# First half of the rows of w1 and w2 by ordinary products; weight sums on VectorE; pairs of rows in turns

## The chip, the core and the metric

One core of a Trainium2 chip. The metric is device microseconds of one execution, the median of three timed runs. PE is TensorE's matmul, PEld its weight load, DVE VectorE, ACT ScalarE, POOL GpSimd, SP the engine that issues the DMAs.

## What is computed

Causal attention (2 batches, 12 heads, 448 tokens, head size 64), then two feed-forward blocks without a nonlinearity in the first and with a squared ReLU in the second:

```python
attn = softmax(mask(q @ k.T / sqrt(64))) @ v      # (2, 12, 448, 64)
x = attn.transpose(0, 2, 1, 3).reshape(896, 768)
a = x @ w1                                        # (896, 1024)
b = x @ w2                                        # (896, 1024)
x = (a * b) @ w3 @ w_out                          # (896, 768)
h = x @ w_in2                                     # (896, 2048)
out = maximum(h, 0) ** 2 @ w_out2                 # (896, 768)
```

All weights arrive as 64-bit floats (two 32-bit words each).

## The kernel before

**Number format.** Each fp32 operand is kept as two tiles, a high part (ACT casts it to fp32r) and a low part (DVE or POOL subtracts the high part from the value). A product of 128 contraction rows is three matmuls (high·high, high·low, low·high). A raw 64-bit weight becomes fp32 by one ACT and two DVE instructions (`convert`, L92, L93, L98; in the changed kernel L93, L94, L99) into one of six slots of `xs`; a *unit* (half a row block, 128x384) is then split into one of eight slots of `ring` by an ACT cast (L87) and a DVE subtraction (L96). In the changed kernel these are L88 and L97.

**Stages, in PE's order.** (1) Attention for 12 pairs of heads; in its gaps PE forms w3 @ w_out (`w_half`), collected in `wraw` and written to DRAM. (2) a and b, from `w1` and `w2`: eight row blocks ("rows", 128 outputs each) of either matrix. (3) `h`: (a*b) times the product of stage 1. (4) Four groups, each of four rows of w_in2 (tiles `win_*`, then `gT`) and of 168 matmuls `o` with w_out2. 

**Stage 2 and the first part of 4 use Strassen's scheme (the form with seven products)** on a pair of rows: contraction halves, and token halves (the two batches) give a 2x2 block problem. A product is nine matmuls of 448 columns (three contraction blocks, three parts). Chains: products 1 and 2 add up in bank a, 6, 7 and 4 in bank b, 5 and 3 in bank c; between two products of one chain DVE reads the bank (L696, L699, L701, L704, L709), so the next product of the chain waits for that read. The weight operands are A11, A12, A22 (units of the rows) and S1 to S4 (sums of halves of rows); the x operands are the blocks B11, B21, B22 and T1 to T4 (sums of B blocks). Before, POOL makes S1 to S4 of a pair with four instructions (`sums`, L240, L241, L243, L244) into two further slots of `xs`, so that a pair takes four of the six slots.

**Order.** PE follows `plan`, in which `TWO` gives the order of the 14 products of two pairs (P of w1, Q of w2; or two pairs of w_in2). `pump` fills the queues of the other engines by a count of what is free: a unit is made as soon as the ring slot of the eighth unit before it has been read for the last time. In stages 2 to 4 a scheduler orders ACT, DVE and POOL; each of them then works strictly in that order. Raw weights come through two buffers (`raw`), so a load starts when the raw tile two before it has been turned into fp32.

Of the kernel before, what the change touches and what calls it, by code (L numbers as in the profile page):

```python
# [8 lines left out]
F32 = mybir.dt.float32  # L9
# [8 lines left out]
def attention_moe_moe2(ctx: ExitStack, tc: tile.TileContext, qk, v, w1, w2, w3, w_out, w_in2, w_out2, out):  # L18
# [25 lines left out]
    LEAD = 5  # L44
    TAIL = 1
    LENT = (("wout", 2), ("wout", 3))
    PAUSE = 64
# [36 lines left out]
    def convert(a=None, y=None, b=None, t=None, x=None):  # L84
# [12 lines left out]
        if a:  # L97
            nc.vector.scalar_tensor_tensor(  # L98
                y.bitcast(U32), y.bitcast(U32), 3, low, op0=ALU.logical_shift_left, op1=ALU.bitwise_or)  # L99

    def halves(x):
# [18 lines left out]
    plan = []  # L120
# [5 lines left out]

    for d in range(KF // 2):
        two_pairs([("w1", 2 * d), ("w2", 2 * d)])
# [21 lines left out]
    def wide(u):  # L150
        return u[0] in ("W", "wout2")
# [14 lines left out]
    def needs(u):  # L166

        if wide(u):
            return u, slice(0, DM)
        name, (nm, m) = u  # L170
        lo, hi = slice(0, HN), slice(HN, DM)
        return {
            "A11": ((nm, m), lo), "A12": ((nm, m), hi), "A22": ((nm, m + 1), hi),
            "S2": (("S12", nm, m), lo), "S1": (("S12", nm, m), hi),
            "S3": (("S34", nm, m), lo), "S4": (("S34", nm, m), hi),
        }[name]

    items, readers = [], {}
    for u in units:
        key = u if wide(u) else u[1]  # L180
        if wide(u):
            group = [u]
        else:
            nm, m = key
            group = [(nm, m), (nm, m + 1), ("S12", nm, m), ("S34", nm, m)]
# [5 lines left out]
        if not wide(u):  # L191
            for it in group[:2]:
                for s in group[2:]:
                    if s not in readers[it]:
                        readers[it].append(s)

    n_unit = {u: i for i, u in enumerate(units)}

    def done_with(it):

        return max(n_unit[r] if r in n_unit else done_with(r) for r in readers[it])

# [31 lines left out]
    def sums(it):  # L234
        which, nm, m = it
        p, q = in_slot((nm, m)), in_slot((nm, m + 1))
        t = in_slot(it)
        a, b = t[:, :HN], t[:, HN:]
        if which == "S12":
            nc.gpsimd.tensor_tensor(b, q[:, :HN], q[:, HN:], op=ALU.add)  # L240
            nc.gpsimd.tensor_tensor(a, b, p[:, :HN], op=ALU.subtract)  # L241
        else:
            nc.gpsimd.tensor_tensor(a, p[:, :HN], q[:, :HN], op=ALU.subtract)  # L243
            nc.gpsimd.tensor_tensor(b, p[:, HN:], in_slot(("S12", nm, m))[:, :HN], op=ALU.subtract)  # L244

    def simple_items():

        while (it := next_item()) and it[0] not in source:
# [7 lines left out]
            items_made.add(it)  # L256
            made["item"] += 1

    def item_of():
# [5 lines left out]
        items_made.add(it)  # L265
        return {"a": it, "y": in_slot(it)}

    def unit_of(at):
# [4 lines left out]
        it, cols = needs(u)  # L273
        if it not in items_made:
            return {}
# [34 lines left out]
    with (  # L310
# [7 lines left out]
    ):  # L318
        wraw = attw.tile([P, KF, DM], F32, tag="W", name="wraw")
        ident = attc.tile([P, P], F32, tag="ident", name="ident")  # L320
# [106 lines left out]
        def x_parts(p):  # L427
# [11 lines left out]
            elif (b, h) == (1, 0):  # L439
                two_parts(xB["B11"][:, 0, k], xB["B11"][:, 1, k], x)  # L440
                xf["T2", k] = f_tile(f"xT2_{k}")
                nc.vector.tensor_tensor(xf["T2", k], x, xf["T3", k], op=ALU.add)
                t1 = xf["T1", k] = xf.pop(("B12", k))
                nc.vector.tensor_tensor(t1, t1, x, op=ALU.subtract)
            else:
# [10 lines left out]
        def w_half(g, i, n):  # L456
# [3 lines left out]
            for f in range(NB):  # L460
# [8 lines left out]
            dst = wraw[:, i, cols]  # L469
            if g > 0:  # L470
                nc.vector.tensor_tensor(dst, acc, dst, op=ALU.add)
                if n == 1:
                    nc.sync.dma_start(out=w_dram[i], in_=wraw[:, i])
            else:
# [242 lines left out]
    more_blocks("x", xB)  # L717
    for n in ("T2", "T1", "T3"):
        for k in range(KH):
            x = xf[n, k] if n == "T2" else xf.pop((n, k))  # L720
            block_parts(xB, n, k, x, nc.gpsimd if n == "T3" else None)
    for k in range(KH):
        x = xf.pop(("B21", k))
        block_parts(xB, "B21", k, x)
        t2 = xf.pop(("T2", k))
        nc.vector.tensor_tensor(t2, x, t2, op=ALU.subtract)
        block_parts(xB, "T4", k, t2)

# [44 lines left out]
    def g_out(nm, m, b, x, in_psum):  # L773
# [49 lines left out]
    w12 = Pairs(xB, ab_out)  # L823
    gs = None
    with tc.manual_schedule(engines={ET.PE}):
        pump(-1)
        for at, (kind, what, which, used) in enumerate(plan):
            if kind == "product":
                nm, m = which
# [74 lines left out]
```

## Time and profile before

| | |
|---|---|
| median of three timed runs | 587.75 us (583.67 to 588.22) |
| profiled execution | 585.41 us, of which 583.6 us from the first to the last instruction |
| PE busy | 546.6 us (94%) |
| DVE, ACT, POOL busy | 406.8, 312.4, 282.0 us (70%, 54%, 48%) |
| mean granted TensorE clock | 0.982 of 2.4 GHz |
| stage 1, attention with w3 @ w_out | 0 to 166.90 us |
| stage 2, products of w1 and w2 | 166.90 to 292.34 us |
| stage 3, h | 292.34 to 350.70 us |
| stage 4, four groups of win and o | 350.70 to 580.3 us |

A stage begins at PE's first matmul of it. PE being busy 94% of the span is an average: stage 3 has no gap at all, stage 2 has its gaps at the seams and between products of one chain. Which gaps these are, and what ended them, stands in the timeline of PE.

### The profile page before, as it was taken

Reading aid. Unit: us, or ns where it says so; the run is one execution under the profiler, and the core shown is the slowest. Engines: PE = TensorE matmul, PEld = TensorE weight load, DVE = VectorE, ACT = ScalarE, POOL = GpSimd, SP = SyncE. Lnnn points to the kernel's source line nnn. Section 1 sums busy time; section 2 is a strip of 40 time slices with the busy share of each in tenths; the row PEclk is TensorE's granted clock in tenths of the full one; section 3 lists DMA queues with packets and bytes.
Section 4 is the critical chain, followed back from the end, with each engine's and each line's share of the span. In section 5 each row is a group of like instructions: output and inputs, shape, how many; then the busy total and the mean of one; then the engine's idle time right before and its main releaser. Section 6 shows DMA issues by size and latency. Waiting matters only on the chain.

```text
span 583.6 us, 8340 instructions
## 1 busy us (share of the span) xinstructions
PE 546.6 (94%) x3004; PEld 485.7 (83%) x3004; DVE 406.8 (70%) x770; ACT 312.4 (54%) x685; POOL 282.0 (48%) x231
## 2 busy tenths in 40 slices
PE   7899989999948988989999999989989998999997
PEld 5668768778837977888999999889989997999997
DVE  5987887878559998787533658863896489538622
ACT  6788777667566453534322546942683258315900
POOL 3378667766535583847253462651164206511510
PEclk9999999999987999898999999999999998999999
DMA  8854554544343333242430304630443045303022
GB/s 298 299 192 137 175 157 156 141 168 125 142 135 107 111 108 109 77 140 83 135 109 0 109 0 116 210 108 1 151 173 108 1 157 169 109 0 109 1 81 110
DMA packets 18153, 70.27 MB, mean 120 GB/s; under 512 B 1920, under 2 KB 4224, under 8 KB 18112
## 3 DMA queue, kind: packets, MB, share of 16 engines
q1 hardware_dynamic: 18112, 69.74, 36.3%
q8 instruction: 24, 0.39, 0.3%
q14 instruction: 17, 0.14, 0.1%
HBM read 63.83 MB, written 5.90 MB: 119 GB/s over the span
## 4 chain that ended last, share of the span: by engine, by line
PE 59%; DVE 15%; ACT 10%; DMA 6%; POOL 5%; issue 4%; DVEq 0%; ACTq 0%; POOLq 0%
PE o L65 18%; PE h L65 10%; PE w L65 8%; DVE ring L96 4%; DVE xs L98 3%; PE s L65 3%; DMA raw_wout<-in_w_out 3%; ACT xs L92 3%; PE x L65 2%; PE pp L408 2%; ACT p L380 2%; ACT pt L412 2%; PE w_6b L65 2%; PE w_4b L65 2%; DMA raw_w<-in_w 2%
## 5 line engine op out<-in xcount | busy, mean ns | idle before, releaser
L96 DVE TENSOR_TENSOR ring<-xs,ring 128x384 fp32r<-128x384 f32 (+1 forms) x140 | 118.4, 858 | 34.4 <-ACT ring L87 34.2
L87 ACT CAST ring<-xs 128x384 fp32r<-128x384 f32 (+1 forms) x140 | 78.4, 577 | 96.9 <-PE o L65 44.9
L390 POOL TENSOR_SCALAR p<-p,st 112x448 f32<-112x448 f32 (+1 forms) x84 | 95.7, 1156 | 53.8 <-ACT pt L412 20.6
L65 PE MATMUL o<-ring,gT 128*128 128x384 f32 x672 | 117.9, 335 | 2.6 <-POOL gT L69 2.6
L65 PEld LDWEIGHTS o<-ring,gT 128*128 128x128 f32 x672 | 116.5, 188 | 3.6 <-POOL gT L69 3.3
L240 POOL TENSOR_TENSOR xs<-xs 128x384 f32<-128x384 f32 x16 | 18.9, 1181 | 98.7 <-DVE ring L96 80.8
L380 ACT ACTIVATE p<-p,st 112x448 f32<-112x448 f32 (+1 forms) x96 | 49.7, 530 | 27.8 <-DVE st L373 27.6
L65 PE MATMUL h<-abT,ring 128*128 128x448 f32 x288 | 58.5, 365 | 0.0
L65 PEld LDWEIGHTS h<-abT,ring 128*128 128x128 f32 x288 | 54.1, 188 | 4.3
L811 DVE TENSOR_TENSOR acc<-o,acc 128x384 f32<-128x384 f32 x42 | 21.4, 550 | 35.1 <-PE o L65 35.0
L373 DVE CUSTOM_DVE_ANT_0 p<-s,mask 112x448 f32<-112x448 f32 (+1 forms) x96 | 36.5, 443 | 6.9 <-PE s L65 6.9
L65 PE MATMUL w<-hl_wout,w 128*128 128x384 f32 x192 | 36.2, 340 | 0.9 <-ACT xB L447 0.9
L92 ACT ACTIVATE xs<-raw_w 128x768 f32<-128x768 f32 (+1 forms) x30 | 24.6, 819 | 20.5 <-DVE ring L96 13.3
L65 PEld LDWEIGHTS w<-hl_wout,w 128*128 128x128 f32 x192 | 32.9, 188 | 2.4 <-ACT xB L447 1.1
L65 PE MATMUL s<-qk 64*112 64x112 f32 (+3 forms) x192 | 28.5, 432 | 4.5 <-DMA qk<-in_qk 4.4
L98 DVE SCALAR_TENSOR_TENSOR xs<-xs,raw_w 128x768 uint32<-128x768 uint32 (+1 forms) x30 | 27.1, 904 | 5.8 <-ACT xs L92 5.7
L408 PE MATMUL pp<-ident,p 112*112 112x112 f32 x240 | 27.4, 262 | 3.7 <-DVE st L373 2.9
L408 PEld LDWEIGHTS pp<-ident,p 112*112 112x112 f32 x240 | 23.6, 134 | 7.9 <-POOL p L390 2.8
L92 ACT ACTIVATE xs<-raw_wout 128x768 f32<-128x768 f32 x24 | 22.0, 925 | 13.7 <-DMA raw_wout<-in_w_out 11.6
L412 ACT COPY pt<-pp 112x336 f32<-112x336 f32 (+1 forms) x72 | 27.7, 477 | 1.8 <-PE pp L408 1.8
L65 PEld LDWEIGHTS s<-qk 64*112 64x112 f32 x192 | 15.9, 185 | 15.1 <-issue 6.0
L65 PE MATMUL w<-ring,w 128*128 128x384 f32 x144 | 27.9, 343 | 0.3 <-DVE w L96 0.3
(307 smaller groups left out, 1078.8 us busy)
## 6 DMA issues: line engine op xcount, KB each, us to landing
raw_wout<-in_w_out SPq DMA_DIRECT2D x24, 768.0 KB, 4.4
raw_w<-in_w SPq DMA_DIRECT2D x16, 768.0 KB, 4.4
raw_win<-in_w_in SPq DMA_DIRECT2D x16, 768.0 KB, 4.3
raw_w<-in_w SPq DMA_DIRECT2D x16, 512.0 KB, 4.2
qk<-in_qk SPq DMA_DIRECT2D x12, 448.0 KB, 5.1
w_dram<-wraw SPq DMA_DIRECT2D x8, 384.0 KB, 3.3
xs<-w_dram SPq DMA_DIRECT2D x8, 384.0 KB, 3.4
v<-in_v SPq DMA_DIRECT2D x12, 224.0 KB, 3.3
```

The costliest lines, as they stand in the source:

```text
L65: return nc.tensor.matmul(o, l, r, start=start, stop=stop, **more)
L87: nc.scalar.copy(t[0], x)
L92: nc.scalar.activation(y, high.bitcast(F32), AF.Prelu, scale=2.0 ** -112, alpha=-2.0 ** 32)
L96: nc.vector.tensor_tensor(t[1], x, t[0].bitcast(F32), op=ALU.subtract)
L98: nc.vector.scalar_tensor_tensor(y.bitcast(U32), y.bitcast(U32), 3, low, op0=ALU.logical_shift_left, op1=ALU.bitwise_or)
L240: nc.gpsimd.tensor_tensor(b, q[:, :HN], q[:, HN:], op=ALU.add)
L373: nc.vector.tensor_tensor_reduce(e, ps[j, i], mask[:, S - (i + 1) * CP:], QS, 3.0e38, ALU.add, ALU.min, st_t[p][:, 0, j, i:i + 1],)
L380: nc.scalar.activation(e, e, AF.Exp, bias=st_t[p][:, 0, j, i:i + 1], scale=-1.0, accum_out=st_t[p][:, 1, j, i:i + 1])
L390: engine.tensor_scalar(e, e, st[:, 3, i:i + 1], None, ALU.mult)
L408: nc.tensor.transpose(x[:CP, o:o + CP], pt[:, off[i] + c * CP:off[i] + (c + 1) * CP], ident[:CP, :CP],)
L412: nc.scalar.copy(t[:, coff[g[0]]:coff[g[0]] + o], x[:CP, :o])
L811: nc.vector.tensor_tensor(a, o, a, op=ALU.add)
```

## The change

**Rows.** The first four rows of w1 and of w2 (`ORDINARY = 4`) no longer go through Strassen's scheme: each is multiplied with the four blocks B11, B12, B21, B22 of x, four products of nine matmuls. For the first four rows (w1_0, w2_0, w1_1, w2_1) the products with B11 and B22 come first, for all of them, and those with B12 and B21 after. B12 takes the tile that T4 had; T4 (`xlast`) is made at the last row, in another tile. Rows 4 to 7 stay in pairs.

**Order of products.** `TWO` is now 1P 1Q 6P 6Q 5P 5Q 7P 7Q 3P 3Q 2P 2Q 4P 4Q, for w1/w2 and for w_in2.

**Sums.** DVE makes the four sums of a pair; S3 and S4 overwrite halves of the rows themselves, so a pair takes three slots of `xs`. S4 is made once A11 is in the ring. POOL makes none.

**Smaller edits.** `wraw` is eight tiles. The T blocks of x are made in another order, T1 from the parts of B11 after the attention, and DVE makes the low parts that POOL made for T3. Of the low parts of `gT` DVE makes two of eight in a group, POOL the rest.

```diff
+    ORDINARY = 4
...
-    TWO = ("P1", "P6", "P5", "Q1", "P7", "P3", "Q6", "Q5", "P2", "P4", "Q7", "Q3", "Q2", "Q4")
+    TWO = [x + n for n in "1657324" for x in "PQ"]
...
-    for d in range(KF // 2):
+    rows = [(nm, i) for i in range(ORDINARY) for nm in ("w1", "w2")]
+    for row in rows[:4]:
+        for u, n in zip(row_units(row), ("B11", "B22")):
+            plan.append(("row", n, row, [u]))
+    for i, row in enumerate(rows):
+        u, u2 = row_units(row)
+        if i >= 4:
+            plan += [("row", "B11", row, [u]), ("row", "B12", row, [u])]
+            plan += [("row", "B21", row, [u2]), ("row", "B22", row, [u2])]
+        else:
+            plan += [("row", "B12", row, [u]), ("row", "B21", row, [u2])]
+    for d in range(ORDINARY // 2, KF // 2):
         two_pairs([("w1", 2 * d), ("w2", 2 * d)])
...
-            nc.gpsimd.tensor_tensor(b, q[:, :HN], q[:, HN:], op=ALU.add)
-            nc.gpsimd.tensor_tensor(a, b, p[:, :HN], op=ALU.subtract)
...
-            nc.gpsimd.tensor_tensor(a, p[:, :HN], q[:, :HN], op=ALU.subtract)
-            nc.gpsimd.tensor_tensor(b, p[:, HN:], in_slot(("S12", nm, m))[:, :HN], op=ALU.subtract)
...
+        tt = nc.vector.tensor_tensor
+        tt(t[:, HN:], q[:, :HN], q[:, HN:], op=ALU.add)
+        tt(t[:, :HN], t[:, HN:], p[:, :HN], op=ALU.subtract)
+        tt(q[:, :HN], p[:, :HN], q[:, :HN], op=ALU.subtract)
...
+            if (nm, m) not in s4_made and ("A11", (nm, m)) in hls:
+                p = in_slot((nm, m))
+                nc.vector.tensor_tensor(p[:, :HN], p[:, HN:], in_slot(it)[:, :HN], op=ALU.subtract)
...
-        wraw = attw.tile([P, KF, DM], F32, tag="W", name="wraw")
+        wraw = [attw.tile([P, DM], F32, tag=f"W{i}", name=f"wraw{i}") for i in range(KF)]
...
-        two_parts(*(g_t[m % 4][:, s, b * S:(b + 1) * S] for s in range(2)), r, nc.gpsimd)
+        two_parts(*(g_t[m % 4][:, s, b * S:(b + 1) * S] for s in range(2)), r,
+                  nc.gpsimd if m % 4 < 2 or b == 0 else nc.vector)
...
+                for k in range(KH):
+                    for s, r in ((0, 0), (0, 1), (1, 0)):
+                        mm(o, t[s][:, k * P:(k + 1) * P], xB[what][:, r, k],
+                           not stop and k == 0 and (s, r) == (0, 0), stop and k == KH - 1 and (s, r) == (1, 0))
+                if stop:
+                    ab_out(nm, m, int(b), row_banks.pop((nm, m, b)), True)
```

ACT's queue at the end of the attention, before (x_1833 is the attention output of the last pair but one, the `xs` casts are units of w1 and w2, the pt copies serve the last pair):

```order
L87 CAST ring<-xs 128x384
L92 ACTIVATE xs<-raw_w_1_1632 128x768 [waits DMAHW4_49,DVE_49]
L87 CAST ring<-xs 128x384 [waits Pool_49]
L447 COPY xB_1_1842<-x_1833 128x448 [waits PE_49]
L87 CAST ring<-xs 128x384
L92 ACTIVATE xs<-raw_w_0_1679 128x768 [waits DMAHW7_49]
L87 CAST ring<-xs 128x384 [waits DVE_49]
L412 COPY pt_1867<-pp_0_1868 112x448 [waits PE_49]
```

The same place in the changed kernel:

```order
L88 CAST ring<-xs 128x384
L93 ACTIVATE xs<-raw_w_0_1636 128x768 [waits DMAHW4_49,DVE_49]
L88 CAST ring<-xs 128x384
L467 COPY xB_1_1842<-x_1833 128x448 [waits PE_49]
L88 CAST ring<-xs 128x384 [waits DVE_49]
L93 ACTIVATE xs<-raw_w_1_1683 128x768 [waits DMAHW7_49]
L88 CAST ring<-xs 128x384
L434 COPY pt_1867<-pp_0_1868 112x448 [waits PE_49]
```

The cast ahead of the copy of x no longer waits for POOL; the cast behind the copy now waits for DVE.

PE's first products of stage 2, before (`w1_0a` is bank a of the pair w1 rows 0 and 1; the second name is the block of x):

```order
L65 MATMUL w1_0a_2017<-xB11_72,ring_70 128x448 x9
L65 MATMUL w1_0b_2037<-xT2_1965,ring_70 128x448 x9
L65 MATMUL w1_0c_2053<-xT1_1964,ring_70 128x448 x9
L65 MATMUL w2_0a_2067<-xB11_72,ring_70 128x448 x9
L65 MATMUL w1_0b_2037<-xT3_1966,ring_70 128x448 x9
```

And in the changed kernel (`w1_0_True` and `w1_0_False` are the two banks of row 0 of w1; xT4 is here B12):

```order
L66 MATMUL w1_0_True_2044<-xB11_72,ring_70 128x448 x9
L66 MATMUL w1_0_False_2055<-xB22_73,ring_70 128x448 x9
L66 MATMUL w2_0_True_2065<-xB11_72,ring_70 128x448 x9
L66 MATMUL w2_0_False_2075<-xB22_73,ring_70 128x448 x9
L66 MATMUL w1_1_True_2085<-xB11_72,ring_70 128x448 x9
L66 MATMUL w1_1_False_2095<-xB22_73,ring_70 128x448 x9
L66 MATMUL w2_1_True_2105<-xB11_72,ring_70 128x448 x9
L66 MATMUL w2_1_False_2115<-xB22_73,ring_70 128x448 x9
L66 MATMUL w1_0_False_2055<-xT4_1968,ring_70 128x448 x9
```

Before, the second product needed T2; now the first eight need only B11 and B22.

POOL's queue between the products of the first group of stage 4 and its `o` matmuls, before (`gT0_3` is the last tile that `o` asks for):

```order
L69 TENSOR_TENSOR gT0_0_3292<-r0_1_3446,gT0_0_3292 128x448 [waits Activation_49]
L240 TENSOR_TENSOR xs_71<-xs_71 128x384 [waits DVE_49]
L243 TENSOR_TENSOR xs_71<-xs_71 128x384 [waits DVE_49]
L241 TENSOR_TENSOR xs_71<-xs_71 128x384 [waits Pool_49]
L69 TENSOR_TENSOR gT0_1_3293<-win2_0s1_3306,gT0_1_3293 128x448 [waits Activation_49]
L244 TENSOR_TENSOR xs_71<-xs_71 128x384 [waits Pool_49]
L69 TENSOR_TENSOR gT0_3_3295<-win2_2s3_3431,gT0_3_3295 128x448 [waits PE_49,Activation_49]
L69 TENSOR_TENSOR gT0_2_3294<-win2_2s2_3419,gT0_2_3294 128x448 [waits Activation_49]
```

In the changed kernel:

```order
L70 TENSOR_TENSOR gT0_1_3291<-win2_0s3_3370,gT0_1_3291 128x448 [waits PE_49,Activation_49]
L70 TENSOR_TENSOR gT0_3_3293<-win2_2s3_3389,gT0_3_3293 128x448 [waits PE_49,Activation_49]
L70 TENSOR_TENSOR gT0_0_3290<-win2_0s2_3332,gT0_0_3290 128x448 [waits Activation_49]
L70 TENSOR_TENSOR gT0_2_3292<-win2_2s2_3351,gT0_2_3292 128x448 [waits Activation_49]
L70 TENSOR_TENSOR gT0_0_3290<-r0_1_3475,gT0_0_3290 128x448 [waits Activation_49]
```

The four sums are gone from this queue, and `gT0_3` stands second in it.

## Rows read from the trace of the kernel before

**Rows 1.** The page, part 1: busy us (share of the span) xinstructions

```profile
PE 546.6 (94%) x3004; PEld 485.7 (83%) x3004; DVE 406.8 (70%) x770; ACT 312.4 (54%) x685; POOL 282.0 (48%) x231
```

**Rows 2.** Timeline, PE, stage 2: start us, us, engine, operation, count, idle before

```profile
159.74 2.35 PE L65 MATMUL w<-hl_wout,w 128*128 128x384 f32 x12 [0.90 <-ACT xB L447]
163.71 2.54 PE L65 MATMUL x<-pt,v 112*64 112x448 f32 x16 [1.62 <-ACT pt L412]
166.90 0.43 PE L65 MATMUL w_0a<-ring 128*128 128x64 f32 x2 [0.65 <-ACT xB L447]
...
174.78 0.74 PE L65 MATMUL w_0b<-xT,ring 128*128 128x448 f32 x1 [5.57 <-ACT xT L68]
...
290.51 1.99 PE L65 MATMUL w_6b<-xT,ring 128*128 128x448 f32 x9
292.34 7.86 PE L65 MATMUL h<-abT,ring 128*128 128x448 f32 x38
```

**Rows 3.** Waits of PE: who waited for whom, us in total, times, longest

```profile
PE o L65 <- POOL gT L69: 2.6, 2, 2.3
PE win_10b L65 <- DVE win_10s L701: 2.6, 1, 2.6
PE w_2b L65 <- DVE w_2s L696: 2.4, 1, 2.4
PE w_4b L65 <- DVE w_4s L701: 2.2, 1, 2.2
PE w_2b L65 <- DVE w_2s L701: 2.0, 1, 2.0
```

**Rows 4.** Timeline, PE, stage 4

```profile
350.70 1.99 PE L65 MATMUL win_0a<-hB,ring 128*128 128x448 f32 x9
...
496.09 29.28 PE L65 MATMUL o<-ring,gT 128*128 128x384 f32 x168
525.21 0.33 PE L65 MATMUL win_12a<-ring 128*128 128x64 f32 x2
...
550.98 29.29 PE L65 MATMUL o<-ring,gT 128*128 128x384 f32 x168
```

**Rows 5.** Timeline, all engines, end of the attention

```profile
153.81 0.55 DVE L93 TENSOR_SCALAR raw_w<-raw_w 128x768 uint32<-128x768 uint32 x1
154.28 0.55 DVE L96 TENSOR_TENSOR ring<-xs,ring 128x384 fp32r<-128x384 f32 x1
154.75 0.95 DVE L98 SCALAR_TENSOR_TENSOR xs<-xs,raw_w 128x768 uint32<-128x768 uint32 x1
...
158.74 0.51 ACT L87 CAST ring<-xs 128x384 fp32r<-128x384 f32 x1 [5.75 <-POOL xs L241]
159.16 0.53 ACT L447 COPY xB<-x 128x448 f32<-128x448 f32 x1
```

**Rows 6.** Timeline, all engines, ahead of the wait of w_2b

```profile
207.23 1.34 POOL L244 TENSOR_TENSOR xs<-xs 128x384 f32<-128x384 f32 x1
...
207.74 1.99 PE L65 MATMUL w_2c<-xT,ring 128*128 128x448 f32 x9
...
209.06 0.91 ACT L92 ACTIVATE xs<-raw_w 128x768 f32<-128x768 f32 x1 [1.26 <-POOL xs L244]
...
210.00 1.93 DVE L98 SCALAR_TENSOR_TENSOR xs<-xs,raw_w 128x768 uint32<-128x768 uint32 x1 [1.02 <-ACT xs L92]
...
213.25 0.61 DVE L696 TENSOR_TENSOR w_2s<-w_2b,w_2s 128x448 f32<-128x448 f32 x1
```

**Rows 7.** Lines by form, stage 2: count | busy us, mean ns | idle before

```profile
L96 DVE TENSOR_TENSOR ring<-xs,ring 128x384 fp32r<-128x384 f32 x51 | 42.8, 847 | 5.8 <-ACT ring L87 5.8
...
L69 POOL TENSOR_TENSOR abT<-w_0s,abT 128x448 fp32r<-128x448 f32 x3 | 4.4, 1470 | 1.9 <-ACT abT L68 1.9
...
L69 DVE TENSOR_TENSOR xB<-xB,xB 128x448 fp32r<-128x448 f32 x3 | 4.0, 1396 | 0.0
...
L69 DVE TENSOR_TENSOR xT<-xT,xT 128x448 fp32r<-128x448 f32 x6 | 3.5, 614 | 0.0
```

More of the change, by code (lines that the diff above doesn't have):

```diff
@@ L184, in attention_moe_moe2 @@
             nm, m = key
[L185 removed]
+            group = [(nm, m)] if u[0] in "LH" else [(nm, m), (nm, m + 1), ("S", nm, m)]
         for it in group:
@@ L190, in attention_moe_moe2 @@
         readers[needs(u)[0]].append(u)
[L191 to L195, printed above, removed]
     n_unit = {u: i for i, u in enumerate(units)}
     def done_with(it):
-        return max(n_unit[r] if r in n_unit else done_with(r) for r in readers[it])
+        return max(n_unit[r] for r in readers[it])
     x_free, x_slot, x_before = [-1] * 6, {}, {}
@@ L273, in unit_of @@
         it, cols = needs(u)
-        if it not in items_made:
+        if it not in items_made or (u[0] in ("S3", "S2") and ("S", *u[1]) not in items_made):
+            return {}
+        if u[0] in ("S1", "S4") and u[1] not in s4_made:
             return {}
@@ L468, in w_half @@
                        f == 0 and (s, r) == (0, 0), f == NB - 1 and (s, r) == (1, 0))
-            dst = wraw[:, i, cols]
+            dst = wraw[i][:, cols]
             if g > 0:
@@ L472, in w_half @@
                 if n == 1:
-                    nc.sync.dma_start(out=w_dram[i], in_=wraw[:, i])
+                    nc.sync.dma_start(out=w_dram[i], in_=wraw[i])
             else:
@@ L717, in attention_moe_moe2, with last_block @@
     more_blocks("x", xB)
-    for n in ("T2", "T1", "T3"):
+    xB["B12"] = xB.pop("T4")
+    for n in ("B12", "B21"):
         for k in range(KH):
-            x = xf[n, k] if n == "T2" else xf.pop((n, k))
-            block_parts(xB, n, k, x, nc.gpsimd if n == "T3" else None)
+            block_parts(xB, n, k, xf[n, k])
     for k in range(KH):
[L723 to L727, printed above, removed]
+        t1 = xf.pop(("B12", k))
+        for s in range(2):
+            nc.vector.tensor_tensor(t1, t1, xB["B11"][:, s, k].bitcast(F32), op=ALU.subtract)
+        block_parts(xB, "T1", k, t1)
+    for n in ("T3", "T2"):
+        for k in range(KH):
+            block_parts(xB, n, k, xf[n, k])
+    for k in range(KH):
+        xf.pop(("T3", k))
+        t2 = xf["T2", k]
+        nc.vector.tensor_tensor(t2, xf.pop(("B21", k)), t2, op=ALU.subtract)
+    def last_block():
+        xB["T4"] = xt.tile([P, 2, KH, S], F32R, tag="T4", name="xlast")
+        for k in range(KH):
+            block_parts(xB, "T4", k, xf.pop(("T2", k)))
     ab = g_tiles("abT", KF)
@@ L827, in attention_moe_moe2 @@
         for at, (kind, what, which, used) in enumerate(plan):
-            if kind == "product":
+            if kind == "row":
+                nm, m = which
+                b, stop = what[2] == "1", (nm, m, what[2] == "1") in row_banks
+                if not stop:
+                    row_banks[nm, m, b] = bank(f"{nm}_{m}_{b}")
+                o, t = row_banks[nm, m, b], hls[used[0]]
+                if at == 0:
+                    pause(o, t)
+                for k in range(KH):
+                    for s, r in ((0, 0), (0, 1), (1, 0)):
[3 more added lines that the diff above has]
+                    ab_out(nm, m, int(b), row_banks.pop((nm, m, b)), True)
+                if at + 1 < len(plan) and plan[at + 1][0] == "product":
+                    last_block()
+            elif kind == "product":
                 nm, m = which
```

26 lines of the change are left out of this document (15 added, 11 removed).

## The prediction, made before the changed kernel had run

> **What bounds the kernel now.** I read the page's busy shares first: PE 94%, every other engine at 70% or less [rows 1]. Time can therefore come only from fewer matmuls or from PE's gaps, and this change adds matmuls. Second, the timeline of PE, for where the gaps are; third, the list of PE's waits, for what ended them; fourth, the timeline of all engines ahead of two of these waits, for what was late behind the engine named.
>
> The reader is to see three kinds of gap. (a) At the end of the attention PE waits 0.90, 1.62 and 0.65 us, each time for ACT, and after the first product 5.57 us for the T2 block [rows 2]. (b) Inside stage 2 and in the win products it waits 2.0 to 2.6 us at a time for DVE to read a bank that the next product of the chain wants (L696, L701) [rows 3]. (c) In the first `o` it waits for a `gT` tile from POOL [rows 3].
>
> Behind (a) and (b) stands POOL. The ACT cast of 158.74 had waited 5.75 us for a weight sum, and the copy that PE's wait of 0.90 us is for stands behind it in ACT's queue [rows 5]. In (b), product 6 of the pair w_2 was through at about 207.7 (the next row of PE begins at 207.74), but DVE read its bank at 213.25 only: POOL's last sum held an `xs` slot to 208.57, ACT's conversion waited for that slot and ran to 209.97, and the DVE half behind it took 1.93 us instead of 0.95 [rows 5, 6]. The lag is 213.86 less 207.7, or 6.1 us, where the old order leaves two products, 3.65 us, of cover.
>
> **The pace without gaps.** One product takes 292.34 − 290.51 = 1.83 us [rows 2]; I use 1.825. A win of 14 products with no wait takes 550.98 − 525.21 = 25.77 us, an `o` of 168 matmuls 525.21 − 496.09 = 29.12 us [rows 4].
>
> **Stage 2, cost.** Before, 56 products; now 8 rows x 4 products and 28 products of pairs, 60. At the pace above 60 x 1.825 = 109.5 us. It took 292.34 − 166.90 = 125.4 us. So four more products cost 7.3 us, and if every gap goes stage 2 gains 15.9 us.
>
> Do they go? The first eight products need B11 and B22 only, which the attention has finished; they last 14.6 us. Their eight units come from four raw rows, as many as the old order had loaded by the same place. B12 and B21 need six casts and six low parts (0.614 us each [rows 7]): under 8 us, inside the cover. The wait of 5.57 us and the slow products behind it (3 us instead of 1.8) go. In the ordinary rows no bank is read between products but at a row's end, with eight banks in turn; nothing of a chain is left to wait for. In the 28 products of pairs the order now puts three products, 5.5 us, between 6 and 7 and between 5 and 3, and five between 7 and 4. A lag of 6.1 us would still stall 0.6; but the sum that made that lag is no longer POOL's and needs no fourth slot.
>
> **DVE is what could spoil it,** since it takes POOL's sums and all x parts. From the order of the changed kernel I count its work in the 58.4 us of the 32 row products: 12 raw starts at 0.55, 10 conversions at 0.95, 20 units at 0.55 [rows 5], 27 subtractions of 448 columns at 0.614 [rows 7], 8 multiplications from PSUM at 0.61 (as L696 [rows 6]), 8 sums. A sum on DVE isn't in the trace: below, it costs what the unit of the same 384 columns costs undisturbed, 0.55; above, that unit's mean in stage 2, 0.847 [rows 7]. I take 0.55, since POOL has no sums left to disturb it. That is 6.6 + 9.5 + 11 + 16.6 + 4.9 + 4.4 = 53.0 us of 58.4. In the 51.1 us of the 28 pair products: 4 starts, 4 conversions, 18 units and 4 double ones, 8 sums, 22 reads of PSUM: 38 us. It fits, narrowly in the rows, where units are made up to eight products (14.6 us) ahead.
>
> The other bound: POOL still works on `abT` in these stretches, 8 and 12 instructions of 1.47 us [rows 7]. Beside POOL a DVE subtraction took 1.396 us instead of 0.614 [rows 7]. If DVE stood still for all of POOL's time, the stretches would need 53.0 + 11.8 = 64.8 and 38 + 17.6 = 55.6 us: 6.4 and 4.5 us too many, 10.9 together.
>
> The Trainium skill, page "SBUF — State Buffer", section "Who interferes with whom", says that a DVE instruction with two SBUF inputs and a GpSimd one that reads SBUF exclude each other, the later one blocked for the whole of the other. By that rule the full 10.9 us would apply; the rows agree that DVE is held (1.396 against 0.614), and do not show whether for the whole instruction.
>
> I take 1.5 us of remaining waits, near the lower end, because of the eight products of lead.
>
> **The start of stage 2.** In the order shown ACT's cast ahead of the copy of x waits for nobody, so the copy comes when x is there, and the pt copies move up with it; the three waits of [rows 2], 3.2 us, go. Between 0 and 3.2 I take 3.2: the raw rows were there, and POOL's sum was the only thing late. The first product now waits for DVE's last addition into `wraw`, which stands behind the conversion of the fourth row; that is done as x ends. SP's loads keep their places.
>
> **Stage 4.** From 350.70 to 525.21 three groups took 174.5 us; three without a wait take 3 x (25.77 + 29.12) = 164.7. The difference, 9.8 us, is what there is to gain. The waits for L701 are between 7 and 4 of one pair, where the order now puts five products, 9.1 us, instead of two. The wait of `o` is for `gT0_3`, which stood behind four sums of POOL; now it stands behind none. DVE takes over six to eight sums and two low parts a group, about 6 us, most of it under the 29 us of `o`, where it mostly adds `acc`. I take all 9.8.
>
> **No time.** The eight `wraw` tiles: DVE's copies and additions wait only for PE in either order, and the block that lies on `wraw` still waits for the last write. Stage 3 has no gap and keeps its 58.4 us; its cover is that units of win are converted as the last tiles of h are read, as before. Stage 1 ahead of 150 us loses three DVE instructions under busy PE.
>
> **Sum,** against the profiled execution's 585.4: −3.2 − 15.9 − 9.8 + 1.5 = 558.0 us. The median of the timed runs is 2.3 above that execution and the lowest 1.7 below; I leave the forecast where the sum is and put that into the range.
>
> **Rivals.**
> 1. *DVE bound.* DVE is held for all of POOL's time in stage 2, or a sum costs more, and it comes late by up to 10.9 us: 585.4 − 28.9 + 10.9 = 567.4. For it: 53 of 58.4 us leaves little, and [rows 7] show means of 0.847 for 0.55. Against: those means were taken with POOL busy with 28 sums more. The skill's rule above is this rival. Chance 0.15.
> 2. *Stage 4 keeps its waits.* DVE's in-order queue holds raw starts that wait for a DMA ahead of a bank's read, and the added sums put it later by more than the new order gives: 558.0 + 9.8 = 567.8. For it: the same DVE queue made those waits. Against: 9.1 us of cover against a lag of at most 6.1. Chance 0.10.
> 3. *Slower.* Beside POOL every DVE instruction of the row stretch is stretched as the three of 1.396 us were, by 2.27. All but the 4.9 us of PSUM reads would then take 48.1 x 2.27 = 109 instead of 48 us; 114 − 58.4 = 56 late, less 14.6 of lead, 41: 558 + 41 = 599. It decides from a factor of about 2.1, where the loss passes the 28.9 us gained. Against: POOL would have to be busy throughout, and has 11.8 us of work there. Chance 0.04.
> 4. *The seams stay.* T blocks or raw rows are late again and only the 7.3 us and part of the gains come: within 1% of 585. Chance 0.04.
>
> **How the numbers follow.** The case of the sum has 0.67, with its own range 553 to 563 (the 1.5 us gone and a fast run; or twice 1.5 and a slow run). Rivals 1 and 2 lie at 567 to 568, both within 571 with the spread of runs. 553 to 571 so holds about 0.85 of the chance, and leaves rivals 3 and 4 and both of 1 and 2 together outside. Within 1% (about what a measurement of this kernel can tell from no change) is rival 4, slower is rival 3: faster 0.92, same 0.04, slower 0.04.
>
> **What would show it.** First product at 163 to 164 us, no wait of PE behind it before the first pair; 58 us for the rows; h beginning near 275; no wait for L701's successor in stage 4; POOL below 220 us busy in all. The forecast is wrong if PE waits for a unit of the ring (rival 1), if PE's waits in win are still above 1 us, or if the granted clock drops in stage 2 with no gap ahead of it.

## The result, and the profile after

The changed kernel takes 561.35 us (median of 4 runs, 557.54 to 565.03) against 586.99 of the kernel before: ratio 0.957, 95% interval 0.950 to 0.965. A second set of six runs, beside other experiments, gave 558.55 us (555.70 to 559.78), ratio 0.954 (0.951 to 0.957). The forecast was 558.0, with 553 to 571 as its range.

The profiled execution took 560.76 us, 24.6 less than the 585.4 of before. Part 1 of its page, busy us (share of the span) and instructions, answers to [rows 1]:

```profile
PE 545.8 (98%) x3040; PEld 486.4 (87%) x3040; DVE 398.8 (71%) x809; ACT 309.7 (55%) x678; POOL 177.1 (32%) x150
```

PE does 36 matmuls more and is busy as long as before, in a span that is 24.6 us shorter. POOL fell from 282 to 177 us, and VectorE, which took over work, from 406.8 to 398.8. The timeline of PE (start us, us, engine, operation, count) answers to [rows 2, 4]:

```profile
158.31 2.34 PE L66 MATMUL w<-hl_wout,w 128*128 128x384 f32 x12
160.58 2.11 PE L66 MATMUL x<-pt,v 112*64 112x448 f32 x16
162.64 0.43 PE L66 MATMUL w_True<-ring 128*128 128x64 f32 x2
...
222.48 3.88 PE L66 MATMUL w_4a<-xB,ring 128*128 128x448 f32 x18
...
274.56 59.68 PE L66 MATMUL h<-abT,ring 128*128 128x448 f32 x288
334.08 2.02 PE L66 MATMUL win_0a<-hB,ring 128*128 128x448 f32 x9
...
500.60 0.33 PE L66 MATMUL win_12a<-ring 128*128 128x64 f32 x2
...
526.36 29.29 PE L66 MATMUL o<-ring,gT 128*128 128x384 f32 x168
```

None of these rows has an idle time noted behind it. The first product comes at 162.64 (166.90 before), stage 2 takes 274.56 − 162.64 = 111.9 us (125.4), stage 3 takes 59.5 (58.4), and the three groups of stage 4 take 500.60 − 334.08 = 166.5 us (174.5). The list of PE's waits from 150 us on (us in total, times, longest) has one line left, where [rows 3] is a choice from many:

```profile
PE o L66 <- DVE win_4s L729: 1.3, 1, 1.3
```

At the end of the attention, ACT's cast that had waited 5.75 us for a weight sum [rows 5] waits for nothing, and the copy behind it (of the last pair but one, as in [rows 5]) comes when PE has made x:

```profile
152.22 2.11 PE L66 MATMUL x<-pt,v 112*64 112x448 f32 x16
...
152.57 0.53 ACT L88 CAST ring<-xs 128x384 fp32r<-128x384 f32 x1
...
154.37 0.53 ACT L467 COPY xB<-x 128x448 f32<-128x448 f32 x1 [1.27 <-PE x L66]
```

Not all that went from stage 2 was idle time. The windows of the kernel before, one for each two pairs of 14 products (start and end; us; busy us and count of PE, PEld, DVE, ACT, POOL; granted clock, DMA share, GB/s):

```profile
166.90:204.00 37.10, 29.76 (x128) 26.07 (x129) 32.41 (x50) 19.25 (x38) 20.99 (x15) 0.86 0.36 117
204.00:236.00 32.00, 27.60 (x128) 24.65 (x127) 28.92 (x37) 13.59 (x27) 20.94 (x17) 0.95 0.31 99
236.00:266.40 30.40, 27.61 (x127) 24.65 (x126) 25.59 (x33) 13.07 (x25) 19.19 (x16) 0.95 0.31 104
266.40:292.50 26.10, 26.10 (x128) 24.14 (x127) 16.36 (x22) 11.01 (x20) 12.59 (x10) 0.98 0.40 121
```

At 1.825 us a product 14 products are 25.6 us of work, but PE was busy for up to 29.8. Part of the time it ran at the lower of its two clock levels (1.2 GHz, a granted clock of 0.50): the products behind the waits of 5.57, 2.02 and 2.21 us took 3.2 to 3.4 us instead of 1.99. (Behind one of 2.38 us, at 213.92, the product took 2.09.) Over the stage PE was idle for 14.5 us and took about 8 us more for its 56 products than at the pace of 1.825; the four added products cost 7.3 us. In the changed kernel the granted clock is 1.00 throughout, so the time that the clock gave back about pays for the four products, and the gain is about what was idle.

**Term by term** the two profiled executions of the same changed kernel stand so against the sum (us, differences to before's own profiled execution):

| | predicted | first profile | second profile |
|---|---|---|---|
| start of stage 2 | −3.2 | −4.3 | −2.7 |
| stage 2 | −15.9 (+1.5 of waits) | −13.5 | −15.7 |
| stage 3 | 0 | +1.2 | 0.0 |
| three groups of stage 4 | −9.8 | −8.0 | −7.6 |
| whole | 558.0 | 560.76 | 559.38 |

In the second, stage 2 takes 109.8 us, where 60 products at 1.825 make 109.5. That the first needs 111.9 with no wait is a matter of PE's pace, and comes below.

### The profile page after: what moved, and what is told of

Its sections match the earlier page's. It is cut to its first block, busy times and chain, and to the rows that moved or that the text cites. A ratio compares the mean times of both kernels' runs of the same rounds, so it can differ in the third digit from the quotient of the medians.

```text
span 559.0 us, 8336 instructions
## 1 busy us (share of the span) xinstructions
PE 545.8 (98%) x3040; PEld 486.4 (87%) x3040; DVE 398.8 (71%) x809; ACT 309.7 (55%) x678; POOL 177.1 (32%) x150
## 4 chain that ended last, share of the span: by engine, by line
PE 85%; DVE 6%; ACT 5%; DMA 3%; issue 1%; DVEq 0%; ACTq 0%
PE o L66 21%; PE h L66 11%; PE w L66 10%; PE w_True L66 5%; PE w_False L66 5%; PE s L66 3%; PE x L66 3%; PE pp L430 3%; PE w_6b L66 2%; PE w_4b L66 2%; ACT p L402 2%; DVE xs L99 2%; ACT pt L434 1%; PE w_6a L66 1%; PE w_6c L66 1%; PE w_4a L66 1%
## 5 line engine op out<-in xcount | busy, mean ns | idle before, releaser
L88 ACT CAST ring<-xs 128x384 fp32r<-128x384 f32 (+1 forms) x128 | 73.2, 583 | 92.0 <-PE o L66 40.3
L97 DVE TENSOR_TENSOR ring<-xs,ring 128x384 fp32r<-128x384 f32 (+1 forms) x128 | 95.3, 754 | 25.6 <-ACT ring L88 25.0
L402 ACT ACTIVATE p<-p,st 112x448 f32<-112x448 f32 (+1 forms) x96 | 49.8, 534 | 25.9 <-DVE st L395 25.6
L66 PE MATMUL h<-abT,ring 128*128 128x448 f32 x288 | 59.7, 368 | 0.0
L70 POOL TENSOR_TENSOR abT<-a,abT 128x448 fp32r<-128x448 f32 x10 | 12.9, 1296 | 65.1 <-ACT abT L69 65.1
L66 PE MATMUL w_True<-xB,ring 128*128 128x448 f32 x144 | 32.3, 369 | 0.0
L66 PEld LDWEIGHTS w_True<-xB,ring 128*128 128x128 f32 x144 | 27.0, 188 | 2.7
L66 PEld LDWEIGHTS s<-qk 64*112 64x112 f32 x192 | 15.8, 184 | 14.5 <-issue 6.0
```

Source lines behind the costliest of these rows:

```text
L66: return nc.tensor.matmul(o, l, r, start=start, stop=stop, **more)
L70: (engine or nc.vector).tensor_tensor(lo, x, hi.bitcast(F32), op=ALU.subtract)
L88: nc.scalar.copy(t[0], x)
L97: nc.vector.tensor_tensor(t[1], x, t[0].bitcast(F32), op=ALU.subtract)
L402: nc.scalar.activation(e, e, AF.Exp, bias=st_t[p][:, 0, j, i:i + 1], scale=-1.0, accum_out=st_t[p][:, 1, j, i:i + 1])
```

## Experiments

The question was which part of the change took out which gap. The prediction said: POOL's sums were late, so their move, with the cover that the new order gives, empties stage 2 and stage 4; the ordinary rows hide the T blocks. All ratios are to the kernel before on the same chip (its medians there: 585.25, 585.50 and 584.36 us). Each row below is a profiled execution (us; "groups" are the three of stage 4).

| kernel | first product | stage 2 | stage 3 | groups | median | ratio (interval) |
|---|---|---|---|---|---|---|
| before | 166.90 | 125.4 | 58.4 | 174.5 | 586.99 | 1 |
| sums on VectorE | 164.84 | 119.5 | 58.4 | 172.0 | 574.53 | 0.981 (0.977 to 0.984) |
| and the order in turns | 168.38 | 112.9 | 58.4 | 168.2 | 567.78 | 0.970 (0.967 to 0.972) |
| changed, second set | 164.18 | 109.8 | 58.4 | 166.9 | 558.55 | 0.954 (0.951 to 0.957) |
| changed, POOL's sums | 163.19 | 111.9 | 59.5 | 173.0 | 567.14 | 0.970 (0.966 to 0.973) |
| changed, old order | 162.97 | 109.8 | 58.4 | 170.2 | 562.09 | 0.961 (0.958 to 0.964) |
| changed, both undone | 164.90 | 109.8 | 58.4 | 173.4 | 566.46 | 0.967 (0.963 to 0.972) |
| changed, two rows each | 163.25 | 109.1 | 59.5 | 164.9 | 556.39 | 0.951 (0.948 to 0.954) |

**Sums alone.** The new order alone can't be built on the kernel before: with four `xs` slots a pair, two pairs in turns want eight of six. So the sums went first:

```diff
-            nc.gpsimd.tensor_tensor(b, q[:, :HN], q[:, HN:], op=ALU.add)
+        tt = nc.vector.tensor_tensor
+        tt(t[:, HN:], q[:, :HN], q[:, HN:], op=ALU.add)
```

> The kernel before with one part of the change: the four sums of a pair on VectorE, in place, three xs slots a pair; the old order of products, no ordinary rows. Theory (POOL's sums were what was late behind most of PE's waits): the 3.2 us at the end of the attention go, the 5.6 us for the T2 block stay, most of the 2.0 to 2.6 us waits of PE in stage 2 and in win shrink under 1 us; about 566 us, ratio 0.965. Rival (the two products of cover of the old order were what was missing, whoever makes the sums): the waits for the bank stay at 1.5 us or more, 578 us or above. Rival (DVE bound): DVE's work in stage 2 of 56 products, with all sums, is late, and PE waits for units of the ring; 585 or above.

574.53 us: neither theory's number. Stage 2 gained 5.9 of the 15.7 us. The run changes two things at once, the engine of the sums and the slots of a pair (three instead of four). The longest waits of PE that are left (us in total, times, longest):

```profile
PE w_0b L65 <- ACT xT L68: 4.1, 1, 4.1
PE w_2b L65 <- DVE w_2s L703: 3.4, 1, 3.4
PE o L65 <- DVE ring L96: 1.6, 2, 1.3
PE win_2b L65 <- DVE win_2s L708: 1.5, 1, 1.5
PE w_4b L65 <- DVE w_4s L703: 1.5, 1, 1.5
```

The T block is still late, and banks are still read late with no sum on POOL: who makes the sum was at most a part of the lag. At the end of the attention the move did help: the first product came 2.1 us earlier.

**Sums and order.** As above, and

```diff
-    TWO = ("P1", "P6", "P5", "Q1", "P7", "P3", "Q6", "Q5", "P2", "P4", "Q7", "Q3", "Q2", "Q4")
+    TWO = [x + n for n in "1657324" for x in "PQ"]
```

> As the run with sums on VectorE alone, and the pairs also in turns, product by product; so the changed kernel without the ordinary rows (and without the eight wraw tiles). Theory: the waits for banks go but for a rest; stage 2 is 56 products, 102.2 us, plus what the T blocks are late (5.6 to 8.6 us), so 108 to 111 us, as long as with the rows: about 561 us, ratio 0.957. If the rows do more than hide the T blocks (DVE has fewer sums and bank reads in them), stage 2 takes 115 us or more and the kernel 567 or above. If the rows cost more than they hide, 557 or below.

567.78 us; the order is worth 6.8 us on top of the sums. Stage 2 took 112.9 us, between the two cases of the forecast (108 to 111, and 115 or more). Its 56 products are 102.2 us of work; the rest is two waits and products at the lower clock (granted clock 0.95 over the stage), and neither wait is for a T block:

```profile
PE w_2b L65 <- DVE ring L96: 3.1, 1, 3.1
PE w_0b L65 <- DVE w_0s L703: 2.2, 1, 2.2
```

The second is for the read of a bank, which ended 7.8 us behind its product (6.1 in [rows 6]), with no sum on POOL. The first product is at 168.38, later than in any other. The timeline of ACT, DVE and PE there:

```profile
166.79 0.56 DVE L237 TENSOR_TENSOR xs<-xs 128x384 f32<-128x384 f32 x1
...
167.38 0.51 ACT L87 CAST ring<-xs 128x384 fp32r<-128x384 f32 x1 [2.96 <-DVE xs L237]
167.80 0.52 ACT L454 COPY xB<-x 128x448 f32<-128x448 f32 x1
...
168.38 0.43 PE L65 MATMUL w_0a<-ring 128*128 128x64 f32 x2 [3.71 <-ACT xB L454]
```

It is the picture of [rows 5] with VectorE in POOL's place: ACT's queue holds the cast of a sum ahead of the copy of x. In the changed kernel the first sum on VectorE is at 193.07 us, because rows need none. So moving the sums, as the prediction had it, opens the seam in part with the old order (2.1 us) and not at all with the new one; rows that need no sum open it whoever makes the sums: with POOL's sums the first product comes at 163.19 and 164.90.

**Sums back on POOL**, in the changed kernel:

```diff
-        tt = nc.vector.tensor_tensor
+        tt = nc.gpsimd.tensor_tensor
```

(and the same for the fourth sum).

> The changed kernel with one word undone: its sums run on POOL again (in place, three slots, new order, rows). Theory (POOL's sums are late): units of the pairs come late, PE waits for the ring or for banks in stage 2's pairs and in win, 571 us or above, POOL busy 225 us or more. Rival (the order's cover of three to five products is enough for whoever makes them): no wait above 1 us, 560 to 563 us.

567.14 us, 571 or more expected and 560 to 563 by the rival. Both are wrong, since the stages answer differently: stage 2 has no wait and takes what it took in the first profile, 111.9 us, though a sum takes 1.0 to 1.4 us there on POOL instead of 0.55; all is lost in the groups. The waits of PE behind the first product, and the place of the longest:

```profile
PE o L66 <- POOL gT L70: 4.1, 3, 2.2
PE o L66 <- DVE ring L97: 1.3, 1, 1.3
```

```profile
415.36 1.73 POOL L252 TENSOR_TENSOR xs<-xs 128x384 f32<-128x384 f32 x1
...
417.06 1.32 POOL L253 TENSOR_TENSOR xs<-xs 128x384 f32<-128x384 f32 x1
...
418.35 1.85 POOL L70 TENSOR_TENSOR gT<-win_4s,gT 128x448 fp32r<-128x448 f32 x1
...
420.25 1.97 PE L66 MATMUL o<-ring,gT 128*128 128x384 f32 x5 [2.24 <-POOL gT L70]
```

Two sums for the next group's products stand in POOL's queue ahead of the low part that `o` needs now.

**The old order**, in the changed kernel (the line `TWO` as before).

> The changed kernel with the old order of the 14 products of two pairs; rows and sums on VectorE stay. Theory (the lag of a bank's read, up to 6 us, needs the three to five products that the new order gives): waits for banks of 1 to 3 us between 6 and 7 and between 7 and 4 come back in the pairs of stage 2 and in win; 566 to 569 us, since the order was worth 7 us where it was added to the sums without rows. Rival (the rows have already taken the pressure off VectorE): stage 2 as in the changed kernel, and only win's waits come back, 563 to 564.

562.09 us, 3.5 above the second set of the changed kernel: the rival. Stage 2 has no wait (109.8); in win the banks are late again:

```profile
PE win_6b L66 <- DVE win_6s L721: 1.6, 1, 1.6
PE win_2b L66 <- DVE win_2s L721: 1.4, 1, 1.4
```

**Both undone.** So the rows alone might be what empties stage 2.

> The changed kernel with its sums on POOL and the old order of the 14 products, both at once; so the ordinary rows are what is left of the change in stage 2 (the sums stay in place, three slots a pair). Each of the two undone alone left stage 2 as it was in the changed kernel. Theory A (the rows alone take the gaps out of stage 2: everything is made so far ahead that the pairs never catch up): stage 2 without a wait again, 109.8 us at the fast pace, the losses of win add up (o behind POOL about 6, win's banks about 3.5): 567 to 570 us. Theory B (either the order or VectorE's sums is needed, as the prediction had it: the lag behind POOL's sum was 6.1 us against 3.65 of cover): waits of 1 to 2.5 us in each pair of stage 2 come back, 573 us or above.

566.46 us, and stage 2 again without any wait, 109.8 us: theory A, half a us below its range. Its timeline shows why neither the new order nor sums on VectorE are needed there (of the rows `w_4b`, those of 225.41 and 234.53 are products 6 of the two pairs, those of 230.89 and 241.83 the products 7 that want their banks):

```profile
225.41 1.99 PE L66 MATMUL w_4b<-xT,ring 128*128 128x448 f32 x9
...
227.51 0.62 DVE L716 TENSOR_TENSOR w_4s<-w_4b,w_4s 128x448 f32<-128x448 f32 x1
...
230.89 1.98 PE L66 MATMUL w_4b<-xT,ring 128*128 128x448 f32 x9
...
234.53 1.99 PE L66 MATMUL w_4b<-xT,ring 128*128 128x448 f32 x9
...
238.39 0.62 DVE L716 TENSOR_TENSOR w_4s<-w_4b,w_4s 128x448 f32<-128x448 f32 x1
```

From the end of a product 6 (the next begins at 227.24 and 236.36) to the end of its bank's read it is 0.9 and 2.6 us, not the 6.1 of [rows 6], and the two and three products of the old order (3.65 and 5.5 us) cover it. In the kernel before the same two products 6 had lags of 4.3 and 4.7 us; the first of them:

```profile
238.07 1.99 PE L65 MATMUL w_4b<-xT,ring 128*128 128x448 f32 x9
239.90 1.99 PE L65 MATMUL w_4c<-xT,ring 128*128 128x448 f32 x9
...
243.62 0.61 DVE L696 TENSOR_TENSOR w_4s<-w_4b,w_4s 128x448 f32<-128x448 f32 x1
```

So the lag was no constant of POOL's sum. In the kernel before it was 2.1 and 3.8 us in the first two pairs, then 6.1 and 4.7, 4.3 and 4.7, and 1.4 and 0.8 in the last two. It goes with VectorE's load: by the windows above VectorE was busy 87, 90, 84 and 63% of these four stretches, and in the last run 79% of the rows (46.3 of 58.7 us) and 74% of the pairs (37.6 of 51.1). My reading: 32 products that ask for two units of one raw row in four products, and for no sum, let ACT and VectorE run ahead, and the lead lasts to the end of stage 2.

One rival is left. All kernels with rows also keep a pair in three slots of `xs`, and have the x blocks in the new order. Slots were short before: in stage 2 ACT's conversions waited 13.9 us for a slot that VectorE was still splitting and 2.4 us for one that POOL's last sum held, against 5.7 and none in the last run. Three slots without rows do not do it (10.3 and 9.7 us of such waits in the two runs without rows, and lags of up to 7 to 8 us); whether rows with four slots would is not shown.

**Fewer rows.** If the lead is what counts, how much of it is needed?

```diff
-    ORDINARY = 4
+    ORDINARY = 2
```

> The changed kernel with two rows each of w1 and w2 by ordinary products in place of four: 16 products of rows and 42 of pairs, two fewer in all (3.7 us). In the profile of the changed kernel VectorE is through with the x blocks 21 us after the first product and has no idle time for 40 us; 16 products last 29.7 us. Theory (rows are there to carry VectorE over the start, and four of a kind are what it needs): PE waits for units or banks between 192 and 205 us by 4 us or more, and the kernel is no faster than the changed one, 560 to 566. Rival (the last four rows only cost): no wait, 557 to 558.

556.39 us (555.77 to 557.21): nearer the rival, and below its range. PE waits once behind the first product, 1.5 us, for `w_4s`, and stage 2 takes 109.1 us with two products fewer, though from that wait, at 231 us, to 358 us its products ran at the slow pace that comes below. By medians it is 2.2 us faster than the changed kernel beside it, and the two intervals (0.948 to 0.954 and 0.951 to 0.957) overlap, so the gain over the changed kernel is likely and not settled. Of all runs it is the lowest.

**One tile for w3 w_out**, the eight tiles undone (`wraw = attw.tile([P, KF, DM], ...)`).

> The changed kernel with w3 w_out in one tile again; each engine's order of instructions is the same. Prediction on record: nothing. Other: the x blocks that lie where wraw was wait for the last store of the whole tile, not for that of their own eighth; ACT's first cast into such a block, at 167.7 us in the changed kernel, comes 2 to 5 us later, and so does what stands behind it in ACT's queue (raw rows); the 8 products of B11 and B22, 14.6 us, hide it, so 0 to 1 us in all; 557 to 560.

558.71 us, ratio 0.955 (0.951 to 0.958): nothing, as forecast; stage 2 takes 109.8 us.

**Low parts of gT.** All on POOL:

```diff
-                  nc.gpsimd if m % 4 < 2 or b == 0 else nc.vector)
+                  nc.gpsimd)
```

> The changed kernel with all low parts of gT on POOL. Theory (POOL is free of sums and has time, VectorE's late read of the bank of win_4 behind the next group's sums is the one wait of stage 4): the wait of o for that bank in group 1 stays at 1.3 to 1.5 us or shrinks; o's first matmuls wait for POOL's last low part of the group by up to 1.6 us in each of four groups; 558 to 564. If both are free: 557.

560.28 us (558.18 to 562.69), ratio 0.958 (0.954 to 0.962): no difference that these runs can tell. PE's one wait behind the start is that of the changed kernel, 0.7 instead of 1.3 us; `o` waits nowhere for POOL. No gain from the two low parts that VectorE took can be seen.

**The pace.** In the first profile every product from 162 to 360 us takes 1.86 us instead of 1.825, with no wait and at a granted clock of 1.00 (the 2.4 GHz level) throughout. The starts in the trace are 206.67 ns apart there on average (207, 207, 206 in turn) over 952 matmuls of 448 columns, and 202.7 ns on average (203, 202, 199, 207 in turn) from win_4 on. Three runs asked whether that is the code or a state.

> The changed kernel once more, unaltered, on the chip of the three runs beside it, for its spread and its pace. Theory (each time PE begins afresh after a wait or a pause, the row of 448-column matmuls falls into one of two paces, 202.7 or 206.67 ns from start to start, and keeps it until it is broken): the 952 matmuls from the first row to the first o, which nothing breaks, run at one pace, either one; with the slow one 560 to 562 us, with the fast one about 4 us less (952 x 4.0 ns = 3.8 us); the timed runs spread over these 4 us or more. Rival (the slow pace belongs to the code of the rows): the same 206.67 ns from 162 to 360 us in this profile too, and in every run.

The unaltered kernel again: all 952 at 202.66 ns, stage 3 in 58.4 us, median 558.55. The same instructions run at either pace. The timeline of PE in the second profile, to be held against the rows of the first above (18 matmuls 3.81 against 3.88, 288 matmuls 58.53 against 59.68):

```profile
222.86 3.81 PE L66 MATMUL w_4a<-xB,ring 128*128 128x448 f32 x18
...
273.94 58.53 PE L66 MATMUL h<-abT,ring 128*128 128x448 f32 x288
332.30 1.99 PE L66 MATMUL win_0a<-hB,ring 128*128 128x448 f32 x9
```

With pauses, first at twelve places, ahead of the fifth row, each two pairs, each pass of h and win_0 (`pause(h_banks[j, b], [t[0][:, 0]])` and the like):

> The changed kernel with a short matmul of 64 columns (the kernel's own pause) also ahead of the fifth row, of each pair of w1's first product, of the first matmul of each pass of h, and of win_0. Theory (the pace of 206.67 ns a 448-column matmul, in which the changed kernel runs from 162 to 360 us with no wait, is a state that an interruption of the row of weight loads and matmuls ends, as the pause ahead of win_4 seems to do): after one of these the gap falls to 202.6 ns on average, 2 to 4 us less, 557 to 559 us. Rival (the pace is set by something else, say what DMA or the other engines do at the time): every stretch keeps its pace, and the pauses cost their 0.2 to 0.4 us each, 562 to 564 us.

560.59 us (559.50 to 561.59), between the two forecasts. All stretches ran at 202.2 to 202.7 ns, the first too, which has the code of the slow one; so the profile cannot tell whether a pause ends a slow pace. The twelve pauses cost 2.6 us in it (0.7 in stage 2, 1.7 in stage 3, 0.2 at win_0), where the pace can cost 3.8. Then at two places:

> The changed kernel with the 64-column pause at two more places only: ahead of the fifth row and ahead of the first product of pairs (each cost 0.2 to 0.4 us in the run with twelve more). Theory of the two paces: a slow pace drawn at the first row ends at the fifth or at the first pair, and the stretch behind it, h too, runs at 202.7 ns; median 557.5 to 559.5, and a narrower spread than the unaltered kernel beside it. Rival (a pause draws no new pace, or the slow one as often): median and spread as the unaltered kernel's, 0.5 us above.

557.58 us (557.14 to 558.29): the narrowest spread of all, 1.2 us, but its interval (0.951 to 0.956) overlaps that of the unaltered kernel. Last, two rows and five pauses:

> The changed kernel with two ordinary rows each of w1 and w2 in place of four, and a 64-column pause ahead of the first product of each two pairs of stage 2, of h and of win_0. Theory: no row beyond the first four is needed (that run took 556.4 us, with one wait of 1.5 us, and ran at the slow pace from 221 to 353 us in its profile, 583 matmuls x 4 ns = 2.3 us); with the pauses, 0.25 us each, a slow pace ends at the next of them: 554 to 556. Rival (the pauses gain nothing beyond their price): 556.4 to 558.

558.43 us (556.76 to 559.06): the rival, 0.4 us above its range. And its profile speaks against the theory of the pause: behind the pause ahead of win_0 124 matmuls ran at 206.67 ns, where those ahead of it ran at 202.67. A pause, like a wait, begins a stretch afresh, and the new stretch can be the slow one. It was so for the first row in 3 of 11 profiles (the changed kernel's first, POOL's sums, low parts on POOL). What decides it stays open.

## Why the prediction was right, and where its reasons were not

The total was right, and each of its terms within 2.5 us. The reading that PE's gaps, and not its work, were what could be taken, held: 60 products instead of 56, and stage 2 is 13.5 to 15.7 us shorter. But the term of stage 2 says that every gap goes, and it comes out the same whatever empties the stage; that it was right is no evidence for the mechanism, and the mechanism was right only in part. The forecast took the stage's whole length before, and so counted PE's slow products in; it named only those behind the T2 block.

- **Start of stage 2**: −3.2 predicted, −4.3 and −2.7 measured. The reason given was that POOL's sum was late. Moving the sums alone gained 2.1 us; the run with sums on VectorE and the new order still waits there, 3.71 us, for a sum. What helps in the changed kernel is that the rows need none. The wait that the prediction named as new, for VectorE's last addition into `wraw`, it took to be over as x ends. It was in the first profile and in that of the old order; in the other nine profiles of kernels with rows PE waited 0.2 to 1.6 us for it, 1.4 in the second profile of the changed kernel. That term was put at nothing and is not.
- **Stage 2**: the size was right, the cause only in part. The prediction gave the rows the T blocks, and to order and sums together the waits for banks, with "a lag of 6.1 us" against three products of cover. With both undone the lag is 0.9 and 2.6 us and nothing waits. The step that failed is the one that took a lag, measured where VectorE was busy 90% of the time, as a property of POOL's sums: with the sums on VectorE and no rows it reached 7.8 us. Without rows, sums and order do gain 12.5 us of stage 2, so the two ways overlap and their gains do not add.
- **The 1.5 us of residual waits** were put into stage 2, where none came. They are in `o` of group 1. The timeline of the first profile there:

```profile
411.95 1.91 DVE L97 TENSOR_TENSOR ring<-xs,ring 128x768 fp32r<-128x768 f32 x1
...
413.30 1.58 POOL L70 TENSOR_TENSOR gT<-win_4s,gT 128x448 fp32r<-128x448 f32 x1 [0.26 <-ACT gT L69]
413.78 1.51 DVE L252 TENSOR_TENSOR xs<-xs 128x384 f32<-128x384 f32 x1
...
415.21 0.55 DVE L253 TENSOR_TENSOR xs<-xs 128x384 f32<-128x384 f32 x1
415.68 0.55 DVE L94 TENSOR_SCALAR raw_win<-raw_win 128x768 uint32<-128x768 uint32 x1
...
416.15 0.94 DVE L99 SCALAR_TENSOR_TENSOR xs<-xs,raw_win 128x768 uint32<-128x768 uint32 x1
...
417.02 0.61 DVE L729 TENSOR_TENSOR win_4s<-win_4b,win_4s 128x448 f32<-128x448 f32 x1
...
417.69 1.49 PE L66 MATMUL o<-ring,gT 128*128 128x384 f32 x7 [1.30 <-DVE win_4s L729]
```

  Product 4 of that pair was through at about 413.2 (the next row of PE begins at 413.18), and its bank was read at 417.02, behind two sums and a conversion for the next group. That is rival 2's mechanism (added sums in VectorE's in-order queue), at 1.3 us and not 9.8: the queue is late at the last products of a group, where `o` wants the bank next and the order has one product left to put between. Rival 1's mechanism has a part in it: beside POOL's subtractions for `gT` the unit of 411.95 took 1.91 us instead of 0.95, and the sum of 413.78 took 1.51 instead of 0.55. By these rows VectorE lost 1.9 us there, more than the 1.3 that PE waited (an estimate: without the loss the read would have ended before `o` wanted the bank). In the second profile two of the sums took 1.5 us each and PE waited 1.5.
- **Stage 4**: −9.8 predicted, −8.0 and −7.6 measured. The difference is that wait, smaller ones in `o`, and in the first profile win_0 at the slow pace. Here the parts are as the prediction had them: sums off POOL free the low parts of gT (6.1 us of the groups, 173.0 against 166.9), the order covers win's banks (170.2 against 166.9).
- **Rival 1, VectorE as the bound**, did not come in stage 2. The windows of the second profile (rows and pairs: us; busy us and count of PE, PEld, DVE, ACT, POOL; granted clock, DMA share, GB/s):

```profile
164.20:222.90 58.70, 58.70 (x291) 54.43 (x292) 49.28 (x79) 30.52 (x58) 8.07 (x6) 1.00 0.46 154
222.90:274.00 51.10, 51.10 (x254) 47.35 (x253) 41.02 (x62) 23.43 (x43) 19.00 (x14) 1.00 0.32 94
```

  VectorE is busy 49.3 us of 58.7 in the rows (53.0 estimated) and 41.0 of 51.1 in the pairs (38). It is held beside POOL, as the lines by form of stage 2 show in the first profile (count | busy us, mean ns):

```profile
L97 DVE TENSOR_TENSOR ring<-xs,ring 128x384 fp32r<-128x384 f32 x38 | 27.0, 712 | 5.6 <-ACT ring L88 5.6
...
L252 DVE TENSOR_TENSOR xs<-xs 128x384 f32<-128x384 f32 x4 | 4.1, 1031 | 0.0
```

  Of the four sums of a pair this one took 1.03 on average (two of the four at 1.5), and the other three 0.55, as the prediction had taken; a unit took 0.71 (0.847 in [rows 7]). That agrees with the rule of the Trainium skill, page "SBUF — State Buffer", section "Who interferes with whom", cited in the prediction: a VectorE instruction with two SBUF inputs and a GpSimd one that reads SBUF contend. The sum of 413.78 above ended 0.4 us behind the subtraction of POOL that had begun before it, so it was held for most of what was left of that one. But in the 58 us of the rows POOL works only 8 us, and 9 to 10 us of VectorE's time were spare in each stretch, so nothing of it reached PE in stage 2.
- **Stage 3** was to keep 58.4 us. It does at the fast pace, and takes 59.5 at the slow one, which the prediction did not know. 952 × 4.0 ns = 3.8 us is about what the first profile has over the second in stages 2 and 3 together (3.3).
- **Rival 3, slower**, did not come. Its turning point was a factor of 2.0 by the prediction's own numbers (48.1 × 2.02 + 4.9 − 58.4 − 14.6 = 28.9), not 2.1; nothing hung on it.

## What to carry to other kernels

A lag read from a trace belongs to the state of the pipeline at that point: before the slow engine is blamed, read the same lag at other places of the same trace, and ask how loaded the feeding engines are there and what lead the stage started with. A stretch that asks little of the feeding engines (here the first rows by ordinary products, at a price of half a product per row) can buy a lead that makes later remedies unnecessary, and then their gains don't add up. In an in-order queue, look for work for the next stage ahead of what the current one waits for: it cost `o` its waits with the sums on POOL, and a smaller one with the sums on VectorE.

## What the runs showed of the hardware

A stream of 448-column matmuls with a weight load each, never waiting and at a granted clock of 1.00, runs at one of two paces, 206.67 or 202.7 ns from start to start, and mostly keeps it until something breaks the stream. The same code drew either. Matmuls of 384 columns in `o` took 173.3 ns in every profile, where nothing waited and the granted clock was 1.00. Two per cent of pace over 200 us is 4 us, and enough to blur comparisons below 1% of this kernel. The first products of the kernel before also changed pace, to the slow one at about 188 us behind a wait, and back near 202 us in the middle of a stream of 117 without one; so a break is not the only thing that ends it.

POOL's work beside it stretched VectorE's subtractions with both inputs in SBUF, and not those that read a bank. In the kernel before, from 160 us on, the 61 units of 128x384 (L96) with no sum, product or subtraction of POOL beside them took 0.54 to 0.56 us; the 49 beside one took 0.99 on average and up to 1.51. The 80 reads of a bank (L696 to L709, one input in PSUM) took 0.61 to 0.63 in either case.
